# Moving one recurrent group by a slot in two batches of an mLSTM and Fourier-mix kernel

## The chip, the cores and the metric

The kernel runs on one core of one Trainium2 chip. The metric is the device time in microseconds. Three runs of the kernel before took 384.13, 385.11 and 386.57 us, so the median is 385.11 us. The profiled execution took 382.61 us, with a span of 380.7 us.

## The reference

There are two blocks, one behind the other. The first is an mLSTM cell over 4 batches, 8 heads, 768 steps and head size 40. Its result, as 768 rows of 320 features per batch, goes into the second: a Fourier mix over both axes, a normalisation, and an MLP from 320 to 1280 and back with a residual.

```python
for t in range(S):
    m_new = np.maximum(f_gate[:, :, t] + m, i_gate[:, :, t])
    f_stab = np.exp(f_gate[:, :, t] + m - m_new)
    i_stab = np.exp(i_gate[:, :, t] - m_new)
    C = f_stab * C + i_stab * np.einsum('bhd,bhe->bhde', vt, kt)
    n = f_stab * n + i_stab * kt
    y[:, :, t] = sigmoid(o_gate) * (C @ q) / np.maximum(np.abs(n @ q), 1.0)
...
u = x + np.real(np.fft.fft(np.fft.fft(x, axis=1), axis=2))
un = (u - mu) / np.sqrt(var + 1e-06)
return u + np.maximum(un @ w_ch1, 0.0) @ w_ch2
```

## The kernel before, in words

The recurrence is computed in chunks. Each batch has six chunks of 128 steps (c = 0 to 5), and in the batches b = 1, 2, 3 each chunk is cut into two halves of 64 steps. I count batches from one in words: the third batch is b = 2, the fourth b = 3.

All work is put on a list with a slot and a phase, by the function `at`, and is issued in that order: by slot, within a slot by phase. The phases of a slot are EVAC (0), FILL (1), MAIN (2) and FILL_PE (3), plus fractions. So each engine's instruction stream, and that of SP, which issues all loads and stores, is fixed by the list. The engines run their streams in order and wait for each other through semaphores only. A slot is no unit of time: an engine can run ahead of another as far as its waits let it. Batches overlap: while the MLP of one batch runs in the MAIN phases, the recurrence of the next one fills the gaps.

`plan_halves(b, s0)` places the recurrence of a batch from slot s0 on, three slots for each chunk: s = s0 + 3c. The third batch has s0 = 54, the fourth s0 = 86. For a chunk it places:

- loads, six slots ahead: queries and keys (`mlstm_load`, tile qk, three buffers, L518; key and value tile kvt, L520), the matrix of stabilisers W (L529, three buffers, in two transfers) and, in the next slot, the decays Gb (L538). Two slots ahead comes the output gate `so` (L544, four buffers);
- on POOL, two slots ahead, the queries times decays (qg, L563), and one slot ahead the values times weights (vw, L569); in its own slot the mask of W (L578) and the decay of the state (C, L705);
- on ACT, one slot ahead, eight exponentials of W (L551, in two halves of four);
- on TensorE (PE) in its own slot, scores and products to the state (tile ps, all through `product`, L582); three slots later the products from the state and from the chunk (tile ph, L582), on ACT a one-element copy behind the first of them (L748) and the tanh of the gate (L650);
- on DVE, in the slot behind, the state's add (L712) and the weighing of the scores (L717), and later `mlstm_finish` (den L768 to L772, x L759).

Because chunk c's last products stand in the same slot as chunk c+1's first ones, PE meets them as one run of L582 instructions: from the state (c), scores and to the state (c+1), from the chunk (c). This is called a group here. Its products use 64 rows or 40 rows of the array. The group for chunks 3 and 4 is the fifth of a batch, counting the one that holds only chunk 0's first products.

The MLP's first layer (`mlp_block`) runs at the same time for the batch before. It works in five sets (i = 0 to 4) of four slots. Step 0 multiplies into the bank p2, step 1 multiplies with T2 into p1, copies p1 to hidden (L1232) and multiplies into p5. Step 2 multiplies into p3, then with T3 into p1, and copies p1 (L1241). Directly behind it, eight products with 64-row tiles (`rest_products`, L1120) add the features that do not fill 128 rows, with adds to hidden on DVE (L1209). Step 3 begins the next set's p1 (L1203, copied by ACT at L1218) and finishes this one's (L1203, ReLU on ACT at L1254). All other products of a set are L1203 and use 128 rows. ReLUs in place are L1258. A product that accumulates into p1 waits for ACT's copy of p1.

The set i = 0 has slots 63 to 66 for the third batch's recurrence and slots 95 to 98 for the fourth's. Its L1120 products are in slots 65 and 97, the two L1203 of step 3 in 66 and 98. In the kernel before, the group of chunks 3 and 4 stands behind step 3.

Stores of finished rows are L1284 and wait for the residual on DVE (L1281). They stand in SP's stream between the loads.

Of the kernel before, what the change touches and what calls it, by code (L numbers as in the profile page):

```python
# [20 lines left out]
NT = S // L  # L21
NP = H // 2
# [35 lines left out]
def kernel(  # L58
# [68 lines left out]
    def at(slot, phase, fn, *args):  # L127
        plan.setdefault((slot, phase), []).append((fn, args))
# [7 lines left out]
    EVAC, FILL, MAIN, FILL_PE = range(4)  # L136
# [682 lines left out]
    def plan_halves(b, s0, stride=3):  # L819
        at(s0 - 2, FILL + 0.7, halves_start, b)  # L820
        for c in range(NT):
            s = s0 + stride * c
            end = c == NT - 1
            t = 22 + 2 * c if b == 1 and c < 3 else s - 6
            at(t, FILL, mlstm_load, b, c)
            at(t, FILL, mlstm_load_max, b, c)
            at(*((t, FILL + 0.02) if (b, c) == (1, 0) else (t + 1 if c < 2 or b > 1 else s - 5, FILL)), mlstm_load_decay, b, c)
            at(s - 2, FILL, mlstm_load_o, b, c)
            at(s - 2, FILL + 0.1, mlstm_scale_q, b, c)
            at(s - 2, FILL + 0.15, halves_alone, b, c)  # L830
            at(*((s - 3, FILL + 0.06) if (b, c) == (1, 1) else (s - 1, FILL)), mlstm_scale_v, b, c)
            early = (b, c) == (1, 0)
            at(*((27, FILL + 0.227) if early else (s - 1, FILL)), mlstm_exp, b, c, 0)
            at(*((28, FILL + 0.23) if early else (s - 1, FILL + 0.5)), mlstm_exp, b, c, NP)
            at(s, FILL, mlstm_mask, b, c)
            at(s, FILL_PE + 2.05, halves_scores, b, c)
            at(s, FILL_PE + 2.5, halves_to_state, b, c)
            for i in range(2):
                at(s + i, FILL + 0.05, halves_decay, b, c, i)
                at(s + 1 + i, FILL - 0.2, halves_add, b, c, i)  # L840
            at(s + 1, FILL, halves_weigh, b, c)
            if end:
                for fn, phase in (((halves_from_state, -0.3), (halves_between, -0.2), (halves_from_chunk, -0.05)) if b == 1 else
                                  ((halves_from_state, 0.1), (halves_between, 0.15), (halves_from_chunk, 0.3))):
                    at(s + (3 if b == 1 else 4), MAIN + phase, fn, b, c)
            else:
                at(s + 3, FILL_PE, halves_from_state, b, c)
                at(s + 3, FILL_PE + 0.5, halves_between, b, c)
                at(s + 3, FILL_PE + 3, halves_from_chunk, b, c)
            at(s + 3, FILL_PE + 0.6, mlstm_tanh, b, c)  # L850
            at(s + 4, FILL + 0.05 if b == 1 else MAIN + 0.4, mlstm_finish, b, c)

# [565 lines left out]
    def plan_batch(b, s_mlstm, s_mix, s_mlp):  # L1420
        if b == 0:
            plan_mlstm(b)
        else:
            plan_halves(b, s_mlstm)
        done = [s_mlstm + n for n in ((17, 19, 22) if b == 0 else (14, 17, 20))]
        assert s_mix >= done[-1] and s_mlp >= s_mix + 9
        late = [s_mlp + 2 * c for c in range(TG)]
        if b == 0:
            feat = [s_mix + 1, s_mix + 1, s_mix + 2]
            turn = [s_mix + 2, s_mix + 3, s_mix + 4]  # L1430
            add = turn + [s_mix + 5, s_mix + 6, s_mix + 7]
            late = [s_mlp, s_mlp + 1, s_mlp + 2]
        else:
            feat = [s_mix + c for c in ((3, 4, 6) if b == 1 else (3, 4, 7))]
            add = [s_mix + c for c in ((4, 4, 5, 6, 7, 7) if b == 1 else (4, 4, 5, 6, 8, 9))]
            turn = [s_mix + c for c in ((5, 6, 6) if b == 1 else (6, 7, 8))]
            late = [s_mix + c for c in ((7, 8, 8) if b == 1 else (9, 10, 10))]
            at(*((s_mlp, EVAC + 0.5) if b == 1 else (s_mlp - 1, MAIN - 0.05)), mlp_sums)
        plan_mix(b, s_mix, done, feat, add, turn + late)
        s = s_mlp + NFF + 2  # L1440
        at(s, FILL + 0.6, mix_rstd, b)
        for n in range(3):
            at(48 + n if b == 0 else s, FILL + 0.65, mix_rstd_step, b)
        plan_mlp(b, s_mlp)
# [22 lines left out]
    for part, (s, phase) in enumerate(((28, 0.1), (28, 0.11), (28, 0.12))):  # L1467
# [3 lines left out]
    early = [(3, mlstm_load, 3), (3, mlstm_load_o, 2), (4, mlstm_load, 4), (5, mlstm_load_decay, 3),  # L1471
             (5, mlstm_load_decay, 4), (7, mlstm_load_o, 3), (7, mlstm_load, 5),
             (11, mlstm_load_decay, 5), (11, mlstm_load_o, 4), (12, load_tables, None), (15, None, 2),
             (11.5, mlstm_load_o, 5)]
# [157 lines left out]
```

## Time and profile before

| | us |
|---|---|
| timed runs | 384.13, 385.11, 386.57 |
| profiled execution | 382.61 |
| its span | 380.7 |
| PE busy | 374.0 |
| DVE busy | 281.9 |
| ACT busy | 170.5 |
| POOL busy | 132.5 |
| L1203, 128-row products of the first layer: mean of one record | 0.506 |
| L1120, 64-row products: mean of one record | 0.497 |
| one exponential L551: mean | 0.337 |

A product in full precision leaves two matmul records, which overlap, so the pace of products is read from the starts of successive ones and not from the durations. PEld is the loading of weights, which overlaps PE. In a listing in order of time, each row has the start, the duration of the merged run, the engine, the line, the operation, what it writes and reads, and how many instructions are merged; in square brackets stands how long the engine was idle before it and what released it. "issue" means that the profile shows no waiting. SPq rows are the issue of a transfer on SP, not the transfer. In a listing by windows, the columns are the busy time of PE, PEld, DVE, ACT and POOL, the granted clock, the busy share of the DMA engines and GB/s.

### The profile page before, as it was taken

What the parts mean: (1) busy time and instruction counts of PE and PEld (TensorE: products, weight loads), DVE (VectorE), ACT (ScalarE), POOL (GpSimd) and SP (SyncE); (2) the same over time, 40 slices, a digit from 0 to 9 for tenths busy, and PEclk for the clock granted to TensorE, in tenths of its full rate; (3) what the DMA queues carried; (4) which work ended last, traced back from release to release, by engine and by line L of the source; (5) the groups of instructions that cost most, each with busy time, mean ns of one, the idle gap of its engine ahead of it and who ended that gap; (6) DMA issues with size and microseconds to landing.
All of it is one profiled execution on the core that took longest, in us unless ns stands there. A gap on an engine that the chain in (4) does not pass through costs nothing.

```text
span 380.7 us, 11406 instructions
## 1 busy us (share of the span) xinstructions
PE 374.0 (98%) x4602; PEld 275.7 (72%) x4602; DVE 281.9 (74%) x662; ACT 170.5 (45%) x501; POOL 132.5 (35%) x238
## 2 busy tenths in 40 slices
PE   8999999999999999999999999999999999999996
PEld 6788555566677777566588999566588996546996
DVE  7798899999998596787955787877844885246552
ACT  5878768557332224654552054564530233544000
POOL 5666424776595014561602434651300000020000
PEclk9999999999999999999999999999999999999999
DMA  7878499879981344464003644430000001000001
GB/s 217 285 217 310 132 250 250 239 232 261 252 211 37 90 127 128 144 179 131 0 3 94 156 117 138 133 69 3 0 2 34 15 22 36 0 0 2 35 36 34
DMA packets 21760, 43.99 MB, mean 116 GB/s; under 512 B 3508, under 2 KB 9996, under 8 KB 21580
## 3 DMA queue, kind: packets, MB, share of 16 engines
q1 hardware_dynamic: 21708, 43.27, 39.0%
q8 instruction: 36, 0.59, 0.6%
q14 instruction: 16, 0.13, 0.1%
HBM read 39.16 MB, written 4.10 MB: 114 GB/s over the span
## 4 chain that ended last, share of the span: by engine, by line
PE 84%; DVE 4%; POOL 2%; DMA 2%; issue 2%; ACT 1%; SPq 0%; POOLq 0%; DVEq 0%; ACTq 0%
PE po L1332 22%; PE pm L1203 19%; PE po L1275 9%; PE pm L1120 7%; PE ph L582 5%; PE pm L1137 4%; PE ps L582 4%; PE pu L990 3%; PE pz L944 2%; PE put L1039 2%; DMA so<-in_o 2%; PE hb L582 1%; PE pzt L944 1%; PE pz L956 1%; DVE stats L1013 1%
## 5 line engine op out<-in xcount | busy, mean ns | idle before, releaser
L1281 DVE SCALAR_TENSOR_TENSOR x<-po,rstd,x 128x160 f32<-128x160 f32 (+1 forms) x69 | 27.1, 394 | 36.6 <-PE po L1332 34.0
L1209 DVE TENSOR_TENSOR h<-h,pm 128x384 f32<-128x384 f32 x60 | 30.5, 549 | 24.7 <-PE pm L1120 11.4
L578 POOL TENSOR_SCALAR_AFFINE_SELECT W<-W 64x512 f32<-64x512 f32 x36 | 27.7, 769 | 38.0 <-ACT W L551 28.6
L1203 PE MATMUL pm<-uT,w_sb 128*128 128x384 f32 x90 | 37.5, 506 | 0.1
L705 POOL TENSOR_TENSOR C<-C,decB 128x164 f32<-128x164 f32 x33 | 19.1, 578 | 52.0 <-DVE C L712 48.7
L551 ACT ACTIVATE W<-W,colT 128x64 f32<-128x64 f32 x144 | 36.6, 337 | 0.0
L1275 PE MATMUL po<-w_sb,h 128*128 128x320 f32 x120 | 33.9, 433 | 0.0
L1120 PE MATMUL pm<-uT,w_sb 64*64 64x384 f32 x320 | 33.7, 497 | 0.0
L563 POOL TENSOR_TENSOR qg<-qk,Gb 128x512 f32<-128x512 f32 x21 | 27.3, 1302 | 8.4 <-DMA Gb<-G_d 7.7
L1063 POOL TENSOR_TENSOR t<-rstd 128x6 f32<-128x6 f32 x12 | 3.7, 312 | 76.1 <-DVE v L1057 75.6
L1275 PEld LDWEIGHTS po<-w_sb,h 128*128 128x128 f32 x120 | 22.4, 190 | 9.1 <-issue 0.3
L1137 PE MATMUL pm<-uT,w_sb 128*128 128x384 f32 x80 | 28.6, 498 | 0.0
L1332 PE MATMUL po<-T,S 128*128 128x160 f32 x180 | 27.8, 301 | 0.2 <-DVE x L1281 0.2
L1332 PEld LDWEIGHTS po<-T,S 128*128 128x128 f32 x180 | 25.4, 190 | 1.3 <-DVE x L1281 0.4
L1332 PE MATMUL po<-w_sb,h 128*128 128x160 f32 x180 | 26.3, 300 | 0.0
L1332 PEld LDWEIGHTS po<-w_sb,h 128*128 128x128 f32 x180 | 25.2, 190 | 1.4 <-DVE x L1281 0.3
L1203 PEld LDWEIGHTS pm<-uT,w_sb 128*128 128x128 f32 x90 | 15.5, 189 | 12.8 <-DVE h L1209 5.3
L1258 ACT ACTIVATE h<-h 128x384 f32<-128x384 f32 x45 | 23.1, 520 | 2.9 <-DVE h L1209 2.9
L1120 PEld LDWEIGHTS pm<-uT,w_sb 64*64 64x64 f32 x320 | 11.4, 132 | 16.9 <-issue 13.7
L1137 PEld LDWEIGHTS pm<-uT,w_sb 128*128 128x128 f32 x80 | 14.2, 190 | 10.5 <-issue 1.8
L569 POOL TENSOR_TENSOR vw<-kvt,colT 128x328 f32<-128x328 f32 x23 | 19.6, 851 | 4.8 <-DVE colT L289 2.5
L582 PE MATMUL ps<-qk 40*64 40x64 f32 (+1 forms) x768 | 19.2, 235 | 0.0
(254 smaller groups left out, 820.4 us busy)
## 6 DMA issues: line engine op xcount, KB each, us to landing
kvt<-in_kv SPq DMA_DIRECT2D x24, 336.0 KB
qk<-in_qkT SPq DMA_DIRECT2D x48, 160.0 KB
raw<-in_w SPq DMA_DIRECT2D x10, 640.0 KB
Gb<-G_d SPq DMA_DIRECT2D x42, 128.0 KB
W<-M_d SPq DMA_DIRECT2D x36, 128.0 KB
so<-in_o SPq DMA_DIRECT2D x24, 160.0 KB
out<-x SPq DMA_DIRECT2D x23, 160.0 KB
ds_sb<-in_dft_s SPq DMA_DIRECT2D x1, 1158.0 KB
```

The costliest lines, as they stand in the source:

```text
L551: nc.scalar.activation(out=k.W[:, h, :], in_=M, func=AF.Exp, scale=-1.0, bias=colT[:, c, 0, b * H + h:b * H + h + 1])
L563: nc.gpsimd.tensor_tensor(out=k.qg[:, :, t], in0=k.qk[:, 0, :, t], in1=k.Gb[:, :, t], op=OP.mult)
L578: nc.gpsimd.affine_select(out=W, in_=W, compare_op=OP.is_ge, fill=0.0, base=base, pattern=[[0, H], [-1 if back else 1, LH]], channel_multi ...
L582: nc.tensor.matmul(out, w, x, start=start, stop=True, skip_group_check=True)
L1120: nc.tensor.matmul(banks[i][half(cols)], w1_rest(n)[half(i), half(cols)], u[half(i)], start=start, stop=not start, skip_group_check=True)
L1137: nc.tensor.matmul(k.pm[i], w1_block(ch, f // 2 * 2 + i), u[2 * ch], start=(ch == 0 and not ahead), stop=(ch == 1 and (ahead or n in (2, 8 ...
L1203: nc.tensor.matmul(bank, w, u, start=start, stop=True, skip_group_check=True)
L1209: nc.vector.tensor_tensor(out=h, in0=h, in1=bank, op=OP.add)
L1258: nc.scalar.activation(out=h, in_=h, func=AF.Relu, scale=-1.0)
L1275: nc.tensor.matmul(k.po[m], hidden(gr, f)[:, i * L:(i + 1) * L], w2_sb[:, f, :], start=(f == 0), stop=(f == NFF - 1))
L1281: nc.vector.scalar_tensor_tensor(out=u, in0=po, scalar=k.rstd[:, c:c + 1], in1=u, op0=OP.mult, op1=OP.add)
L1332: nc.tensor.matmul(po, a[:, f], w[:, f], start=start and f == 0, stop=f == half - 1, skip_group_check=True)
```

## The change

For the third and fourth batch (b > 1) only:

- Chunk 4 (c = NT - 2) goes one slot sooner as a whole (s is one less): its loads, scalings, mask, scores, products to the state and state adds.
- The last products of chunk 3, its tanh and its finish go one slot sooner with it, so that the group of chunks 3 and 4 stays one group. It stands in slot 65 (97), behind the L1120 products and ahead of the two L1203 of step 3. The last products, tanh and finish of chunk 4 keep their old slots.
- The exponentials of chunk 4 go from s - 1 to two slots ahead of its new s, into the FILL_PE phase of slot 63 (95), and those of chunk 5 from slot 68 (100) to four slots ahead, the FILL_PE phase of slot 65 (97).

```diff
-            s = s0 + stride * c
+            s = s0 + stride * c - (b > 1 and c == NT - 2)
             end = c == NT - 1
+            follow = s + 3 + (b > 1) * ((c == NT - 2) - (c == NT - 3))
...
-            at(*((27, FILL + 0.227) if early else (s - 1, FILL)), mlstm_exp, b, c, 0)
-            at(*((28, FILL + 0.23) if early else (s - 1, FILL + 0.5)), mlstm_exp, b, c, NP)
+            ahead = (s - (2 if c == NT - 2 else 4), FILL_PE + 0.7) if b > 1 and c >= NT - 2 else None
+            at(*((27, FILL + 0.227) if early else ahead or (s - 1, FILL)), mlstm_exp, b, c, 0)
+            at(*((28, FILL + 0.23) if early else ahead or (s - 1, FILL + 0.5)), mlstm_exp, b, c, NP)
...
-                at(s + 3, FILL_PE, halves_from_state, b, c)
-                at(s + 3, FILL_PE + 0.5, halves_between, b, c)
-                at(s + 3, FILL_PE + 3, halves_from_chunk, b, c)
-            at(s + 3, FILL_PE + 0.6, mlstm_tanh, b, c)
-            at(s + 4, FILL + 0.05 if b == 1 else MAIN + 0.4, mlstm_finish, b, c)
+                at(follow, FILL_PE, halves_from_state, b, c)
+                at(follow, FILL_PE + 0.5, halves_between, b, c)
+                at(follow, FILL_PE + 3, halves_from_chunk, b, c)
+            at(follow, FILL_PE + 0.6, mlstm_tanh, b, c)
+            at(follow + 1, FILL + 0.05 if b == 1 else MAIN + 0.4, mlstm_finish, b, c)
```

In the streams of the engines this gives, in each of the two batches: on PE the group passes the two L1203 of step 3. On ACT chunk 4's exponentials pass L1232 and stand behind chunk 2's tanh; chunk 3's copy L748 and tanh and then chunk 5's exponentials pass L1218, L1254 and L1258. On POOL qg and vw of chunk 4 pass the decay of chunk 3's second half. On DVE chunk 4's first state add and weighing pass one weight sum, in the third batch only. On SP the Gb loads of chunk 4 pass chunk 3's gate load and, in the third batch, a store too; the gate load of chunk 4 passes the query, key/value and W loads of chunk 5. The numbers of instructions are the same on every engine.

## The prediction

> **What bounds the kernel.** I read the table of busy time first, then the chain that ended last, then the timeline around slots 64 to 69 of the third batch (b = 2) and 96 to 101 of the fourth (b = 3).
>
> ```profile
> span 380.7 us, 11406 instructions
> PE 374.0 (98%) x4602; PEld 275.7 (72%) x4602; DVE 281.9 (74%) x662; ACT 170.5 (45%) x501; POOL 132.5 (35%) x238
> PE 84%; DVE 4%; POOL 2%; DMA 2%; issue 2%; ACT 1%; SPq 0%; POOLq 0%; DVEq 0%; ACTq 0%
> ```
>
> TensorE is busy 98% of the span and holds 84% of the chain; the granted clock is 9 tenths or more in every slice. Listed in order of time, the chain stays on PE from 257.80 us to the end. So the change is worth what it takes from or adds to PE's own sequence. The two places look alike; this is the fourth batch:
>
> ```profile
> 243.55 2.02 ACT L551 ACTIVATE W<-W,colT 128x64 f32<-128x64 f32 x8
> 244.55 2.30 PE L1120 MATMUL pm<-uT,w_sb 64*64 64x384 f32 x16
> 245.47 0.46 ACT L1241 COPY h<-pm 128x384 f32<-128x384 f32 x1
> 245.98 0.20 PEld L1120 LDWEIGHTS pm<-uT,w_sb 64*64 64x64 f32 x6 [0.60 <-ACT h L1241]
> 246.78 0.30 PEld L1203 LDWEIGHTS pm<-uT,w_sb 128*128 128x128 f32 x2 [0.60 <-DVE h L1209]
> 248.27 0.56 PEld L582 LDWEIGHTS ph<-C,qg 40*64 40x64 f32 x32 [0.55 <-issue]
> 249.90 2.00 ACT L551 ACTIVATE W<-W,colT 128x64 f32<-128x64 f32 x8
> 250.15 0.91 PE L1203 MATMUL pm<-uT,w_sb 128*128 128x384 f32 x2
> ```
>
> The reader is to see ACT's order. The eight exponentials of chunk 4 (243.55) stand ahead of the copy L1241. That copy waits only for a product of 243.71, so it could start at about 244.56 (in an undisturbed set the product is at 168.81 and the copy at 169.66, 0.85 later). It starts at 245.47, and the 64-row products L1120 wait for it. Then come two 128-row products, the recurrent group, and the next 128-row product at 250.15. The third batch has the same picture at 160.52 to 166.13.
>
> **What leaves PE's path.** The order of instructions shows one change on PE in each of the two batches: the two L1203 products go from before the group to behind it. Nothing is added or removed on any engine. From the first L1120 to the L1203 that follows all of this, PE now takes 166.13 - 160.52 = 5.61 us and 250.15 - 244.55 = 5.60 us. Afterwards I add: L1120 to the group's first product as where they already stand side by side, 1.34 us (169.55 to 170.89, next fence); the group, 164.24 to 166.13, 1.89; the first 128-row product behind a group, 166.13 to 166.88, 0.75; the second at the running pace, 0.65 (167.52 to 168.17). Sum 4.63, so **0.98 us less in the third batch and 0.97 in the fourth**.
>
> ```profile
> 169.55 1.55 PE L1120 MATMUL pm<-uT,w_sb 64*64 64x384 f32 x16
> 170.89 0.65 PE L582 MATMUL ph<-C,qg 40*64 40x41 f32 x32
> ```
>
> Of it 0.77 is the wait for the copy (L1120 to the next L1203 takes 1.47 in a quiet set, 185.01 to 186.48, here 2.24) and 0.2 the saved change between 128-row and 64-row products. The first part comes from chunk 4's exponentials alone: they go to right behind the tanh of 156.48 (and 240.55), where ACT now idles 2.21 us (2.16) until L1232. They would run 156.95 to 158.97 and 241.0 to 243.0; L1232 is ready at 159.15 and 243.18, so 0.2 us of slack covers them. Their W was issued at 146.18 and 233.44, long before.
>
> For the change of shape the rows give 0.1 us a side: a running product takes 0.64 (168.17 to 168.81), the last one ahead of 64 rows 0.74 (168.81 to 169.55) and the first behind them 0.75, although the weight load idles 0.55 there. One change each way goes per batch.
>
> The Trainium skill (TensorEngine Tiling (Array Packing), Key Properties) says that changing the tiling mode drains TensorE. It states no price; were the drain the whole idle of 0.55, each side would save 0.45 more, 1.8 in both batches, and the sum below would be 383.3. The pace of the products is against it.
>
> **What else moves.** On POOL the query scaling (1.26) and the value scaling (0.74) of chunk 4 pass the decay of chunk 3's second half. They wait for the group of slot 63, which is done with its queries at 156.4; then 157.0 to 159.2, the decay to 159.7, the mask to 161.1. The adds that read this stand at 161.70 on DVE, the group needs the values at about 162.9. Hidden by 1 to 2 us; without that cover the group would wait the difference. DVE's three adds L1209 stand at 161.93 and now have until 163.75, when the first L1203 comes. The add and the weighing of chunk 4 pass a 1.04 us weight sum in the third batch, whose result is first used in the second layer's products, at 193.55. The decay load Gb of chunk 4 is issued ahead of a store and of chunk 3's gate load; the gate is read 10 us later.
>
> **What becomes late.** Chunk 5's eight exponentials go four slots ahead, in front of L1218, L1254 and L1258. They need chunk 5's W. In the same edit the gate load of chunk 4 (L544, 160 KB) goes ahead of chunk 5's query, key/value and W loads on SP. In the third batch, W is issued at 157.79 and the trace's landing semaphores end at 161.39. The exponentials can start at about 163.2 (tanh behind the group's first part). With the gate load ahead, up to 0.85 later, it is still there in time: they end at 165.2, L1218 at 165.6, and the product that needs it (the second of the next set, at 165.8) waits for nothing. The fourth batch differs:
>
> ```profile
> 236.92 5.42 SPq L1284 DMA_DIRECT2D out<-x  x2
> 242.39 0.75 SPq L518 DMA_DIRECT2D qk<-in_qkT  x2
> 243.19 0.35 SPq L520 DMA_DIRECT2D kvt<-in_kv  x1
> 243.70 1.09 SPq L529 DMA_DIRECT2D W<-M_d  x2
> 244.84 0.59 SPq L544 DMA_DIRECT2D so<-in_o  x1
> ```
>
> ```profile
> 245.00:245.50 0.50, 0.50 (x9) 0.19 (x2) 0.47 (x2) 0.50 (x4) 0.00 (x0) 1.00 1.01 254
> 249.00:249.50 0.50, 0.50 (x59) 0.50 (x51) 0.00 (x0) 0.44 (x3) 0.00 (x0) 1.00 0.97 212
> ```
>
> SP sits on a store until 242 (it waits for L1281 on DVE), and only then issues chunk 5's loads, in one burst. The second fence, half-microsecond windows with the DMA share as the last figure but one, shows the DMA engines full from 245 to 249.5. The landing semaphores of W's two halves end at 248.62 and **249.28**, those of the gate load behind them at 250.12. So today's exponentials at 249.90 have W by 0.6 us. Moved, they would reach ACT's head at 247.2 (group from 245.89, its first results 0.8 later, tanh to 247.2) and stand there for W, with L1218 behind them. The gate load put ahead of W adds between 0.4 (its issue alone; 0.42 to 0.59 in the rows) and 0.84 us (what it takes behind W). I take 0.7, near the upper end since the engines are full: W at 249.98. The Trainium skill (DMA: Bandwidth & Descriptors, Queues, rings and completion order) says that each DMA engine consumes descriptors in ring order, so this load delays W; the landing order here agrees, 249.28 before 250.12.
>
> The exponentials take 2.0, the next ACT row starts 0.1 ahead of their end (245.57 against 245.47): L1218 at 251.88, done 252.36, the waiting product at 252.41 (0.05 later, as at 159.63 to 159.68). It now starts at 250.90 and without the wait would start at 249.93. So the wait costs 2.48 and leaves **+1.51 us** there. Some comes back: the next 64-row products now wait for a DVE add (253.57) behind a 1.47 us gate product that POOL's qg slows; L1120 to the L1203 after the next group is 257.73 - 253.57 = 4.16 against 173.15 - 169.55 = 3.60. DVE will have done that gate product before 250, so 0.56 goes. Net **+0.95 in the fourth batch**.
>
> **Sum.** -0.98 + 0.95 = -0.03 us: no change. The profiled execution took 382.61 us (span 380.7), the timed runs 385.11 in the median (384.13 to 386.57), 2.5 above it; on that scale I forecast **385.1**. Bounds: gate load without effect on W, 384.4; 0.84 and nothing of the 0.56 back, 385.8. About 1% (3.9 us) is what a measurement here tells from no change.
>
> **Rivals.**
> - *Chunk 5's W is not late in the fourth batch*: -0.98 - 0.97 - 0.56 = -2.5, 382.6 us. For it: the cost hangs on one burst, and a store issued some 2 us sooner would end it. Against it: 249.28 is 2 us behind 247.2, and DVE's order ahead of the store is unchanged. 0.17.
> - *The backlog is larger (slower)*: the gate load moves at the slowest pace of the burst (139 GB/s at 246.5, 1.2 us for 160 KB), W lands at 250.5, and the 0.56 does not come back as L1254, L1258 and L1232 queue on ACT: -0.98 + 1.51 + 0.5 = +1.0, and with L1232 one copy late (0.5) +1.5, 386.6 us. It decides from a landing after 250.1. 0.2.
> - *No gain from the move*: another wait takes the copy's place (the add L1209 for the first L1203, slack 1.3; L1232 behind the exponentials, slack 0.2). Then -0.98 goes, +1.9, 387.0. Little speaks for it: 0.05.
>
> The forecast has 0.58. The range 382.6 to 387.0 takes in the rivals and the scatter of the runs. None of the cases reaches 3.9 us by itself; for the scatter I leave faster by over 1% 0.05, slower 0.05, within 0.9.
>
> **What would show it.** Right: L1120 in both batches without the 0.60 wait for L1241 and L582 straight behind it; in the fourth batch ACT idle for some 2.7 us ahead of L551 with a DMA named as releaser, and the second product of the next set waiting for ACT. The step on W falls if that idle is missing; the first step falls if L1120 still takes 2.30. The whole is wrong if a wait appears outside these two places, above all in the mixing of the batch.

## The result, and the profile after

The changed kernel is slower by 0.58%: the ratio of its times to those of the kernel before is 1.0058, with an interval of 1.0031 to 1.0085. The median of 20 runs is 386.50 us, that of 20 runs of the kernel before 383.69 us, so the change costs about 2.2 us (1.2 to 3.3). The ratio leaves out a few runs in a second, slower state, so it is not the ratio of these two medians. The three runs from which I forecast had a median of 385.11 us. On the larger set of runs "no change" would have been 383.7 us, so the median lies inside the range of 382.6 to 387.0 us partly because that range stood too high.

The page of the profiled execution after: the span, the busy times, and the shares of the chain that ended last.

```profile
span 384.0 us, 11410 instructions
...
PE 373.0 (97%) x4602; PEld 275.2 (72%) x4602; DVE 281.4 (73%) x662; ACT 170.4 (44%) x501; POOL 132.1 (34%) x238
...
PE 73%; DVE 8%; issue 5%; POOL 3%; ACT 3%; DMA 1%; SPq 1%; POOLq 0%; ACTq 0%; DVEq 0%
```

TensorE does 1.0 us less (373.0 against 374.0), and the span is 3.3 us longer. In the chain, PE's share falls from 84% to 73%; "issue" grows from 2% to 5% and DVE from 4% to 8%. So there are new waits, and not all of them are on a semaphore.

In the code after the change, lines from L1120 on are higher by two: L1120 is now L1122, L1203 is L1205, L1209 is L1211, L1218 is L1220, L1232 is L1234, L1284 is L1286 and L1303 is L1305. In the experiments they are as after, but in e3 higher by one and in e9 by three.

To see where the time goes I take the distances between the first L1120 product of successive MLP sets. In the third batch's recurrence I call the first three sets a, b, c, and in the fourth's d, e, f. Predicted was -0.98 for a to c and +0.95 for d to f.

| us | start of a | a to b | b to c | a to c | d to e | e to f | d to f |
|---|---|---|---|---|---|---|---|
| before | 160.52 | 9.03 | 8.80 | 17.83 | 9.03 | 9.35 | 18.38 |
| after | 162.65 | 8.44 | 9.54 | 17.98 | 10.59 | 8.80 | 19.39 |

The 3.3 us of the span have three parts: 2.13 ahead of a, 0.15 in the third batch and 1.01 in the fourth. From c to d nothing moved (66.20 and 66.19). The fourth batch does what was predicted. The third does not, and nothing was predicted for the part ahead of it.

**The third batch.** The timeline of the kernel after, in order: TensorE and its weight loads.

```profile
162.65 1.52 PE L1122 MATMUL pm<-uT,w_sb 64*64 64x384 f32 x16
164.49 0.56 PEld L582 LDWEIGHTS ph<-C,qg 40*64 40x64 f32 x32 [0.99 <-DVE x L759]
164.50 0.68 PE L582 MATMUL ph<-C,qg 40*64 40x41 f32 x32 [0.32 <-DVE x L759]
166.38 0.91 PE L1205 MATMUL pm<-uT,w_sb 128*128 128x384 f32 x2
171.88 0.21 PEld L1122 LDWEIGHTS pm<-uT,w_sb 64*64 64x64 f32 x8 [0.60 <-DVE h L1211]
```

The 64-row products now run through in 1.52 us instead of 2.30, and the group comes right behind them. But the group starts 1.84 us behind the first L1122, where the sum had 1.34: its first product waits for L759, the end of the finish of chunk 2. And the next set, which was undisturbed before, waits for a DVE add (171.88). The same stretch on DVE and POOL, after, and then four rows of before:

```profile
159.57 1.51 DVE L1193 TENSOR_TENSOR m<-uT,raw 128x384 f32<-128x384 f32 x1
162.93 0.98 DVE L772 SCALAR_TENSOR_TENSOR so<-so,den 128x320 f32<-128x320 f32 x1
163.95 0.49 DVE L759 TENSOR_TENSOR x<-ph,so 128x320 f32<-128x320 f32 x1
166.96 2.10 DVE L1305 TENSOR_TENSOR w_sb<-w_sb 128x800 f32<-128x800 f32 x1
```

```profile
159.09 1.58 POOL L563 TENSOR_TENSOR qg<-qk,Gb 128x512 f32<-128x512 f32 x1
162.21 1.37 POOL L578 TENSOR_SCALAR_AFFINE_SELECT W<-W 64x512 f32<-64x512 f32 x2
166.94 1.27 POOL L563 TENSOR_TENSOR qg<-qk,Gb 128x512 f32<-128x512 f32 x1
```

```profile
157.44 0.56 DVE L1191 TENSOR_TENSOR m<-uT,raw 128x384 f32<-128x384 f32 x1
160.76 0.49 DVE L772 SCALAR_TENSOR_TENSOR so<-so,den 128x320 f32<-128x320 f32 x1
163.34 1.04 DVE L1303 TENSOR_TENSOR w_sb<-w_sb 128x800 f32<-128x800 f32 x1
161.61 1.38 POOL L578 TENSOR_SCALAR_AFFINE_SELECT W<-W 64x512 f32<-64x512 f32 x2 [0.78 <-ACT W L551]
```

Three DVE operations take about twice as long or more, each beside a POOL operation that it did not stand beside before: L1193 takes 1.51 us (before 0.56, with POOL idle from 156.99 to 158.32), the gate product L772 0.98 (before 0.49, with POOL idle from 160.83 to 161.61), the weight sum 2.10 (before 1.04). In the first case the change moved POOL's query scaling there; in the second the mask, which comes sooner because chunk 4's exponentials do; in the third it moved the weight sum itself, on DVE, beside chunk 5's query scaling. All three read two tensors in SBUF. One that reads a tensor from SBUF and the other from a bank that TensorE has written keeps its time: the product L759 takes 0.49 us at 163.95, with POOL idle, and 0.49 at 170.64 beside a mask. The second slow operation delays L759 and so the group; the third delays the adds of the next set.

**The fourth batch.** The timeline of SP, ACT and PE:

```profile
239.20 5.41 SPq L1286 DMA_DIRECT2D out<-x  x2
246.45 1.09 SPq L529 DMA_DIRECT2D W<-M_d  x2
```

```profile
246.82 1.52 PE L1122 MATMUL pm<-uT,w_sb 64*64 64x384 f32 x16
249.57 1.06 PE L582 MATMUL ph<-kvt,W 64*64 64x41 f32 x32
252.20 2.02 ACT L551 ACTIVATE W<-W,colT 128x64 f32<-128x64 f32 x8 [2.62 <-DMA W<-M_d]
254.63 0.91 PE L1205 MATMUL pm<-raw 128*128 128x384 f32 x2 [1.87 <-ACT h L1220]
```

ACT stands idle for 2.62 us until W has landed, and the second product of the next set waits for L1220 behind the exponentials. It starts 7.81 us behind the first L1122; the prediction had 7.86 (252.41 less 244.55). One row was not foreseen: the group's last products (249.57) take 1.06 us instead of 0.66.

**Ahead of both.** A window of the kernel after, between 80 and 90 us, where the instruction streams of both kernels are the same, and below it the same window of before. The columns are the window, its length, the busy time (and instructions) of PE, PEld, DVE, ACT and POOL, the granted clock, the DMA share and GB/s. Then two rows of PE's timeline after:

```profile
80.00:90.00 10.00, 8.19 (x156) 4.83 (x154) 7.58 (x15) 3.30 (x9) 6.15 (x9) 1.00 0.75 209
80.00:90.00 10.00, 10.00 (x166) 5.75 (x168) 9.50 (x18) 5.28 (x16) 7.25 (x10) 1.00 0.79 229
```

```profile
81.32 1.50 PE L1122 MATMUL pm<-uT,w_sb 64*64 64x384 f32 x10 [0.63 <-issue]
87.75 0.54 PE L582 MATMUL ph<-kvt,W 64*64 64x41 f32 x18 [1.18 <-issue]
```

TensorE is busy for 8.19 of 10 us at full clock (before: 10.00). Twice it stops in the middle of a run of products and waits for nothing that the profile shows ("issue").

### The profile page after: what moved, and what is told of

It reads as the page before. It is cut to its first block, busy times and chain, and to the rows that moved or that the text cites. A ratio compares the mean times of both kernels' runs of the same rounds, so it can differ in the third digit from the quotient of the medians.

```text
span 384.0 us, 11410 instructions
## 1 busy us (share of the span) xinstructions
PE 373.0 (97%) x4602; PEld 275.2 (72%) x4602; DVE 281.4 (73%) x662; ACT 170.4 (44%) x501; POOL 132.1 (34%) x238
## 4 chain that ended last, share of the span: by engine, by line
PE 73%; DVE 8%; issue 5%; POOL 3%; ACT 3%; DMA 1%; SPq 1%; POOLq 0%; ACTq 0%; DVEq 0%
PE po L1334 19%; PE pm L1205 16%; PE po L1277 7%; PE pm L1122 6%; PE pm L1139 4%; PE ph L582 4%; PE ps L582 3%; PE pu L992 3%; PE pz L946 2%; PE hb L582 2%; ACT W L551 2%; DMA W<-M_d 1%; PE pzt L946 1%; DVE stats L1015 1%; POOL W L578 1%
## 5 line engine op out<-in xcount | busy, mean ns | idle before, releaser
L1211 DVE TENSOR_TENSOR h<-h,pm 128x384 f32<-128x384 f32 x60 | 30.5, 550 | 27.1 <-PE pm L1205 13.7
L578 POOL TENSOR_SCALAR_AFFINE_SELECT W<-W 64x512 f32<-64x512 f32 x36 | 28.4, 788 | 36.4 <-ACT W L551 25.2
L551 ACT ACTIVATE W<-W,colT 128x64 f32<-128x64 f32 x144 | 36.6, 335 | 2.6 <-DMA W<-M_d 2.6
L1205 PE MATMUL pm<-uT,w_sb 128*128 128x384 f32 x90 | 37.3, 503 | 0.1
L705 POOL TENSOR_TENSOR C<-C,decB 128x164 f32<-128x164 f32 x33 | 18.2, 550 | 49.7 <-DVE C L712 45.4
L1122 PE MATMUL pm<-uT,w_sb 64*64 64x384 f32 x320 | 32.7, 496 | 0.6 <-issue 0.6
L1205 PEld LDWEIGHTS pm<-uT,w_sb 128*128 128x128 f32 x90 | 15.7, 189 | 12.1 <-DVE h L1211 4.1
L1122 PEld LDWEIGHTS pm<-uT,w_sb 64*64 64x64 f32 x320 | 11.1, 132 | 16.8 <-issue 14.5
```

Of the source, the lines that this page charges most:

```text
L551: nc.scalar.activation(out=k.W[:, h, :], in_=M, func=AF.Exp, scale=-1.0, bias=colT[:, c, 0, b * H + h:b * H + h + 1])
L578: nc.gpsimd.affine_select(out=W, in_=W, compare_op=OP.is_ge, fill=0.0, base=base, pattern=[[0, H], [-1 if back else 1, LH]], channel_multi ...
L1122: nc.tensor.matmul(banks[i][half(cols)], w1_rest(n)[half(i), half(cols)], u[half(i)], start=start, stop=not start, skip_group_check=True)
L1205: nc.tensor.matmul(bank, w, u, start=start, stop=True, skip_group_check=True)
L1211: nc.vector.tensor_tensor(out=h, in0=h, in1=bank, op=OP.add)
```

## The experiments

The theory after this reading: the group's gain is halved by DVE being slowed beside POOL; W costs what was predicted; the part ahead of a does not come from the moved work. The rivals: the moved exponentials are the cause; the gate load and not the store makes W late; the moved work reaches back to 80 us in some way. All ratios are to the kernel before, measured on the same chip; distances are of the profiled executions.

**The changed kernel again**, with no edit.

> The changed kernel once more, to separate the scatter from the effect. Theory A: the two distances are 17.98 and 19.39 us again within 0.2, and the median is 1 to 2 us above that of before on the same chip. Rival B: the first L1120 of the third batch is again more than 1.5 us later than in the kernel before (160.52), and the whole 2 us slower or more.

Ratio 1.0090 (1.0049 to 1.0130). Start of a 163.77, a to c 17.98, d to f 19.05. The "issue" stops are there again (1.59 us at 82.16 and 1.17 at 88.60, at the same two instructions). So they are no accident of one execution of this program.

**e1: chunk 5's exponentials at their old place**

```diff
-ahead = (s - (2 if c == NT - 2 else 4), FILL_PE + 0.7) if b > 1 and c >= NT - 2 else None
+ahead = (s - 2, FILL_PE + 0.7) if b > 1 and c == NT - 2 else None
```

> The changed kernel with chunk 5's exponentials back in slots 68 and 100; the rest of the change stays. Theory A (what the two traces show at the two places): the wait of ACT for W in the fourth batch goes, and with it 1.93 us on PE (there the product behind L1220 came 3.73 late after 1.80). Left are +0.15 in the third batch, -0.47 in the fourth and there perhaps -0.55 (a DVE add no longer late), so 0.3 to 0.9 us less than the kernel before. Rival B (the loss sits in the 2.1 us which the profiled execution of the changed kernel was late at 107 us already, ahead of the first moved instruction, and belongs to the change): still 1 to 2 us slower than before.

Ratio 0.9997 (0.9957 to 1.0038); a to b 9.39, d to e 9.96, d to f 18.77. The weight loads of TensorE in the third batch:

```profile
169.92 0.30 PEld L1205 LDWEIGHTS pm<-e,raw 128*128 128x128 f32 x2 [1.29 <-ACT h L1234]
```

With the group sooner, TensorE reaches the next set before ACT has done the exponentials at their old place, and the copy L1234 stands behind them. So this part of the change is needed by the other, where W is there in time: from a to b it is worth 0.95 us in the third batch (9.39 against 8.44). Up to c only 0.21 is left (18.19 against 17.98), since behind the longer wait the late weight sum no longer delays the next set (b to c 8.80). I had expected 0.3 to 0.9 us less than the kernel before, and that did not come.

**e2: the gate load of chunk 4 behind chunk 5's loads again**

```diff
-at(s - 2, FILL, mlstm_load_o, b, c)
+at(s - 2 + (b > 1 and c == NT - 2), FILL, mlstm_load_o, b, c)
```

> The changed kernel with chunk 4's gate load issued behind chunk 5's query, key/value and W loads again, as before the change; chunk 5's exponentials stay ahead. Theory A with the prediction's 0.7 for the gate load: W lands 0.4 to 0.84 us sooner in the fourth batch, and ACT's idle time ahead of L551 there shrinks from 2.62 to about 1.9 (1.8 to 2.2), the time by as much: 0.4 to 0.8 us less than the changed kernel. Rival: the burst is bound by something else, the landing stays, no difference.

Ratio 1.0017 (0.9978 to 1.0055); a to c 17.98, d to f 19.00. ACT idles 2.23 us ahead of L551, with 2.62 in the kernel after and 2.28 when that kernel ran again. Behind the first L1122 the waiting product starts at 7.41 us. In the kernels that leave SP's order here as the change has it, it starts at 7.46 (the changed kernel again), 7.81, 7.86 (e5), 8.26 (e7, below) and 8.94 (the padded kernel, below). The gate load's share, 0.4 to 0.84 us by my estimate, is lost in the scatter of W's landing, and putting it back does not cure the wait.

**e3: the kernel before with chunk 4's exponentials alone moved**

```diff
+ahead = (s - 3, FILL_PE + 0.7) if b > 1 and c == NT - 2 else None
-at(*((27, FILL + 0.227) if early else (s - 1, FILL)), mlstm_exp, b, c, 0)
+at(*((27, FILL + 0.227) if early else ahead or (s - 1, FILL)), mlstm_exp, b, c, 0)
```

(and the same in the line for the other four heads)

> The kernel before with chunk 4's exponentials alone moved to the FILL_PE phase of slots 63 and 95; no group moves. The prediction's step (0.77 us of the 0.98 come from these exponentials alone): 0.77 in each batch, 1.5 us less than before. Theory A (DVE is late as well: the adds L1209 stand behind chunk 2's finish, at 161.93 and 245.98 in the trace of before, whoever is ahead on ACT): the first L1203 still waits until the first of these adds is done, 246.47, so at 246.5 in place of 246.78: 0.25 in each batch, 0.5 less than before.

Ratio 0.9968 (0.9934 to 1.0002); a to b 9.32, so 0.29 longer; d to e 9.13, 0.10 longer; d to f 17.93, 0.45 shorter, all of it in the next set (e to f 8.80). Weight loads and DVE in the third batch:

```profile
162.66 0.30 PEld L1204 LDWEIGHTS pm<-uT,w_sb 128*128 128x128 f32 x2 [1.67 <-DVE h L1210]
```

```profile
160.38 1.00 DVE L772 SCALAR_TENSOR_TENSOR so<-so,den 128x320 f32<-128x320 f32 x1
```

The wait for the copy is gone, and nothing is gained at the place: the two products of step 3 now wait for the adds of the 64-row products, which stand on DVE behind a gate product of 1.00 us. The mask L578, which follows the exponentials, starts at 160.39 here and at 161.61 before. So the gain that I put down to the exponentials alone takes the group's move as well, which gives DVE that time.

**e4 and e5: the change in the third batch alone, and in the fourth alone** (`b > 1` becomes `b == 2`, or `b == 3`, in the three new expressions)

> The whole change in the third batch alone. Prediction: -0.98. Theory A: -0.49 at the group (which waits for chunk 2's finish on DVE) and +0.74 in the next set (whose 64-row products wait for a DVE add behind a weight sum that takes 2.10 in place of 1.04 beside POOL), +0.15 in sum with the rounding of the rows, no difference that can be measured. Rival B: +1 to +2 us, though the fourth batch is as before.

> The whole change in the fourth batch alone. Theory A: the distance from the first L1120 of the batch's first set to that of its third grows from 18.38 to about 19.4 us, 1.0 us slower than before in all. Rival B (the loss belongs to streams ahead of the moved instructions): 2 us slower or no difference, by chance, with the same 1.0 at the place.

e4: ratio 1.0008 (0.9967 to 1.0049), a to c 17.98, d to f 18.48. e5: 1.0040 (1.0001 to 1.0079), a to c 17.83, d to f 19.45. The two places add up (0.15 in e4's third batch and 1.07 in e5's fourth are 1.22, against 1.16 for both), and a starts at 160.37 and 159.83: with either half of the change alone, no time is lost ahead of it. (e1 and e2, which have nearly all of it, lie between: 161.38 and 161.27.)

**e6: chunk 5's loads in the fourth batch one slot sooner, ahead of the second store**

```diff
-t = 22 + 2 * c if b == 1 and c < 3 else s - 6
+t = 22 + 2 * c if b == 1 and c < 3 else s - 6 - ((b, c) == (3, NT - 1))
```

> The changed kernel with chunk 5's query, key/value and W loads of the fourth batch issued ahead of the second of the two stores that SP waits for (and so ahead of chunk 4's gate load). Theory A (W is late only since SP sits on that store until 242 and then issues everything in one burst): W is issued as soon as chunk 2's products release its buffer, lands about 3 us sooner, ACT's idle time of 2.62 us ahead of L551 goes and with it 1.9 us on PE: 18.38 us becomes about 17.5, and the whole is 1.9 us faster than the changed kernel, some 0.8 faster than before. Rival (the DMA engines are full in any case): the idle time stays above 1.5.

Ratio 0.9967 (0.9931 to 1.0003); d to f 17.55, which is 1.84 less than after and 0.83 less than before. SP and ACT in the fourth batch:

```profile
237.07 0.76 SPq L518 DMA_DIRECT2D qk<-in_qkT  x2
...
241.57 1.40 SPq L529 DMA_DIRECT2D W<-M_d  x2
243.06 0.53 SPq L1286 DMA_DIRECT2D out<-x  x1
```

```profile
246.96 2.00 ACT L551 ACTIVATE W<-W,colT 128x64 f32<-128x64 f32 x8
```

W is issued 2.7 us ahead of d (244.30) and no longer 0.4, and the exponentials start without idle time ahead of them. So the wait in the fourth batch came from SP, which sat on a store while the load stood behind it.

**e7: POOL's scaling of chunk 4 back behind the state decay, the third batch's weight sum from slot 66 to 77**

```diff
+own = int(b > 1 and c == NT - 2)
-at(s - 2, FILL + 0.1, mlstm_scale_q, b, c)
+at(s - 2 + own, FILL + 0.1, mlstm_scale_q, b, c)
...
-at(66 if n == 3 else 57, FILL + 0.41, out_weight_sums, n)
+at(77 if n == 3 else 57, FILL + 0.41, out_weight_sums, n)
```

(the same `+ own` for `halves_alone` and `mlstm_scale_v`)

> The changed kernel with POOL's query and value scalings of chunk 4 behind the decay of chunk 3's second half again, as before the change, and the weight sum in slot 77 in place of 66. Theory A (DVE is slowed by POOL beside it, and its lateness takes half of the gain in the third batch and gives a stall in its next set): the last of the four operand sums on DVE (L1193, 1.51 us) is back at 0.56, the group's wait for the finish L759 shrinks from 0.99 to 0.6 or less of the weight load's idle time, the stall of 0.60 in the next set goes, and the distance of the third batch falls from 17.98 to 16.9 to 17.3 us (17.83 before the change). The fourth batch keeps its wait for W. In all 0.7 to 1.0 less than the changed kernel. Rival (the group waits for something else): 17.9 or more.

Ratio 1.0030 (0.9991 to 1.0070). L1193 is back to 0.56 us and b to c to 8.80, so a to c is 17.23, 0.60 less than in the kernel before. But a to b stays at 8.43: the group still waits for L759, because the gate product is still slow beside the mask, now its first half (1.01 us from 160.00, the mask from 160.02). So the slow L1193 cost the group next to nothing; the slow gate product makes the wait. In the slot 77 the weight sum delays another set by 0.3, and in the fourth batch, which still has SP's order, d to f is 19.83.

**The padded kernel: the changed kernel with one more instruction on POOL** (a one-element memset, 0.09 us at 273.8 us, long behind everything in question)

```diff
+at(112, FILL + 0.9, nc.gpsimd.memset, warm[64:65, 2:3], 0.0)
```

> The changed kernel with one more instruction: a memset of one spare element on POOL, near the end of the fourth batch's MLP; TensorE, VectorE, ScalarE and SyncE have the same instructions in the same order. It is to tell whether the microsecond or two that the changed kernel loses ahead of the third batch's recurrence belongs to the moved work. Theory (it does not; it comes from how the program is supplied to TensorE, which any small alteration changes): the distances of the sets stay at 17.98 and 19.0 to 19.4 us, the stalls of TensorE on nothing but the issue between 80 and 90 us are gone or elsewhere, the first set of the third batch's recurrence starts at 159.8 to 161.5 us, and the time is 1 to 1.5 us over the kernel before (ratio 1.002 to 1.004). Rival (the moved work causes it): start at 162.6 to 163.8 us again, stalls at 80 to 90 us again, ratio 1.006 to 1.009.

Ratio 1.0011 (0.9975 to 1.0047). a starts at 160.31, a to c is 17.97, d to f 20.52. The windows of this kernel between 80 and 90 us:

```profile
80.00:90.00 10.00, 10.00 (x170) 6.00 (x172) 9.68 (x19) 5.59 (x16) 7.57 (x10) 1.00 0.79 228
```

TensorE is busy for all of it and the stops are missing, while the third batch shows the same distance. The interval lies just below that of the changed kernel's second run, but overlaps that of its first (1.0031 to 1.0085), so the traces tell the two kernels apart and the times hardly do. They were not on the same chip; but on the chip of that second run e5, e6 and e7 have their a at 159.8 to 160.1, so it isn't the chip alone. The moved work is therefore not enough to make the 2 to 3 us ahead of a: with all of it in place and an instruction more, they are not there in this execution.

The 20.52 missed the expectation of 19.0 to 19.4, because W landed later:

```profile
250.98 2.02 ACT L551 ACTIVATE W<-W,colT 128x64 f32<-128x64 f32 x8 [3.76 <-DMA W<-M_d]
```

From the issue of W to these exponentials it takes 6.90 us here (244.08 to 250.98) and 5.75 in the kernel after (246.45 to 252.20), and the product behind L1220 starts at 8.94 instead of 7.81. PE's rows ahead of it show something else, which costs nothing here, as that product waits longer still:

```profile
247.21 0.52 PE L582 MATMUL ph<-kvt,W 64*64 64x41 f32 x21
248.96 0.43 PE L582 MATMUL ph<-kvt,W 64*64 64x41 f32 x11 [1.23 <-issue]
```

This is the same kind of stop as at 81 and 88 us, inside the moved group. In the fourth batch the step to the 118th of the group's 128 products takes 0.34 us in the kernel after, 0.07 when it ran again, and in e1, e2, e6, e7 and the padded kernel 0.92, 1.18, 0.64, 0.56 and 1.45; in e5 it is 0.03, and the next one 0.07. Before, no step near there is over 0.03. The third batch's group has it in none of these runs, nor has the fourth's where it stands as before (before, e3 and e4). So the stop lies at one place of TensorE's stream, and its length differs. The same holds for the earlier ones: e2 stops for 0.62 us at 86.52, at the very product of the stop at 87.75 in the kernel after. Counting all instructions that the trace has of TensorE in order, the stops at 81.32, 87.75 and in the group are at 2241, 2497 and 7360: 256 and 19 times 256 apart, to within one. A stop of 0.29 us in e1 and e3 (at 105.33 and 104.17) is at 3265, 3 times 256 behind the second.

**e8: both repairs, e6 and e7, together**

> Changed kernel with both repairs: the last chunk's loads of the fourth batch one slot sooner, ahead of the second store, and POOL's products of the fifth group behind its second decay again, with the third batch's sum of output weights moved from slot 66 to slot 77. If the two repairs are independent: first to third set 17.2 us in the third batch (before 17.83) and 17.5 or less in the fourth (before 18.38), 0.3 us lost at slot 77, so 1.2 us less than the kernel before: ratio 0.996 to 0.998. If DVE's or POOL's later work takes the place of the waits in the fourth batch (there W is in time only if POOL's products are too), 18 us or more there and a ratio of 0.999 to 1.001.

Ratio **0.9948** (0.9908 to 0.9988), median 381.63 against 383.80; a to c 16.71, c to d 66.46, d to f 17.41. The third batch is better than expected by 0.5. The next two kernels tell why.

**e8b: as e8, the weight sum in a gap of DVE at the end of slot 82**

```diff
-at(77 if n == 3 else 57, FILL + 0.41, out_weight_sums, n)
+at(*((82, FILL_PE + 1) if n == 3 else (57, FILL + 0.41)), out_weight_sums, n)
```

> As the kernel with both repairs, but the third batch's sum of output weights (0.99 us on DVE) goes to the end of slot 82, where the trace shows DVE idle for 1.33 us behind the last ReLU of the MLP's input and ahead of the hidden sums. Expected: the 0.3 us between the last set and the fourth batch's recurrence comes back (66.2 instead of 66.5), and the rest is as in the kernel with both repairs: 1.5 us less than before, ratio 0.995 to 0.997. If the gap is needed by what follows it, the first output products wait instead, 66.5 us or more again.

Ratio 0.9974 (0.9947 to 1.0000). The 0.3 us from c to d came back (66.19), as expected. But a to c is 17.23 and d to f 17.96. In the fourth batch the stop inside the group is 1.18 us here and 0.62 in e8. In the third the gate product differs; its row in e8 first, then in e8b:

```profile
160.44 0.49 DVE L772 SCALAR_TENSOR_TENSOR so<-so,den 128x320 f32<-128x320 f32 x1
```

```profile
160.57 1.01 DVE L772 SCALAR_TENSOR_TENSOR so<-so,den 128x320 f32<-128x320 f32 x1
```

In both, POOL's mask starts just behind it: 25 ns in e8, 22 in e8b (12 in e3, 20 in e7, and L772 took 1.00 and 1.01 there). In e8 the mask's first half takes 0.98 us, elsewhere 0.65. In the fourth batch, where the mask starts 111 to 116 ns behind the gate product (e3, e7, e8, e8b), the gate product keeps its 0.51 us and the mask's first half takes 0.91. So one of the two is held up by the other, and at 12 to 25 ns a few nanoseconds go with which one.

**e9: as e8b, two one-element memsets on POOL ahead of the mask, third batch only**

```diff
+for i in range(2 * (b == 2) * own): at(s, FILL, nc.gpsimd.memset, warm[64:65, 2 + i:3 + i], 0.0)
 at(s, FILL, mlstm_mask, b, c)
```

> The kernel with both repairs and the sum of output weights at the end of slot 82, and with two one-element memsets on POOL (0.09 us each in the padded run) ahead of the fifth group's mask in the third batch, so that POOL's mask starts some 0.2 us behind DVE's gate product instead of within 0.02 us of it. Theory (whichever of DVE's gate product and POOL's mask starts first holds the other up, and the group's first product waits for DVE's finish behind the gate product): the gate product takes 0.49 to 0.51 us instead of 1.01, and the first to second set of the third batch 7.9 us instead of 8.43, first to third 16.7 instead of 17.2. Rival (the 0.5 us between 7.91 and 8.43 in the two kernels with both repairs comes from the place of the weight sum, or from chance elsewhere): 8.43 us again whatever the gate product takes. Fourth batch as it is, 17.4 to 18.0. Time 1.5 to 2 us less than before, ratio 0.995 to 0.997.

Ratio **0.9950** (0.9908 to 0.9992), median 380.72 against 382.88; a to b 7.91, a to c 16.71, c to d 66.19, d to f 17.41. DVE, POOL and PE in the third batch:

```profile
160.92 0.49 DVE L772 SCALAR_TENSOR_TENSOR so<-so,den 128x320 f32<-128x320 f32 x1
```

```profile
161.25 1.39 POOL L578 TENSOR_SCALAR_AFFINE_SELECT W<-W 64x512 f32<-64x512 f32 x2
```

```profile
160.68 1.52 PE L1123 MATMUL pm<-uT,w_sb 64*64 64x384 f32 x16
162.02 0.65 PE L582 MATMUL ph<-C,qg 40*64 40x41 f32 x32
```

The mask starts 0.33 us behind the gate product, neither is slowed (the mask's halves take 0.67 and 0.66), and the group follows the 64-row products at 1.34 us, as in the sum. The theory's two numbers (7.9 and 16.7) came, and the rival's (8.43) did not. e8 and e9 beat both the kernel before and the changed one; their intervals do not tell one from the other.

## Why the prediction was wrong

I forecast -0.03 us; the interval is +1.2 to +3.3. In the profiled executions the miss is 3.3 us: 1.13 in the third batch (+0.15 in place of -0.98), from the step on POOL and DVE below; 0.06 in the fourth; and 2.13 ahead of both, for which the prediction had no term.

**What leaves PE's path (4.63 us): right as a length, wrong as a forecast.** The product that the sum ends at comes 5.12 us behind the first L1122 in the third batch after (167.77 less 162.65), and 4.59 in e9 (165.27 less 160.68). So the durations were right, 0.1 us for the change of shape included. That speaks against the other value that I weighed: with 0.45 more saved a side, e9 would have come 0.9 sooner. What was missing is the wait of the group's first product. I took its start from a row where DVE had finished long before (170.89). At the new place the finish of the chunk before ends at the very moment that the group arrives, and 0.5 us of DVE decides 0.5 us of the kernel.

**"The first part comes from chunk 4's exponentials alone": wrong.** e3 has them alone, and TensorE waits for DVE's adds instead, 0.29 us longer than before in the third batch and 0.10 in the fourth. The sign stood in the prediction's own rows: the first L1203 (246.78) is released there by DVE's L1209 and not by the copy. This did not move the sum, since the change has both parts.

**"Hidden by 1 to 2 us" (POOL and DVE): the step that failed.** I compared when the moved POOL work had to be done with when it would be done. I did not ask what runs beside it. POOL's query scaling, mask and value scaling now lie beside DVE operations that read two tensors in SBUF, and those took 1.51 instead of 0.56, 0.98 instead of 0.49, and 2.10 instead of 1.04 us. I had the mask end at 161.1, and the gate product stood at 160.76: the overlap was in my own numbers. The price in the third batch is 0.49 at the group and 0.74 at the next set, against a gain of 0.98 and 0.10 that I had not counted (the next set's first product no longer stands behind the group: 0.65 instead of 0.75). The sum is +0.15 in the place of -0.98. The weight sum, which I named as passed and free, was the dearest of them. e7 takes away the second price (b to c 8.80), e9 the first as well (a to b 7.91). The prediction had such a case before it: it says of the next set's gate product that "POOL's qg slows" it, and used this only where it brought a gain.

The Trainium skill (SBUF — State Buffer, SBUF: two separate sides) has the rule: VectorE and GpSimd share a pair of SBUF ports under an exclusive lock, and whichever starts first holds it for the whole instruction, between a VectorE operation with two SBUF inputs and a GpSimd operation that reads SBUF too. The runs agree that one waits for the other: beside the mask the gate product ends about 0.34 us behind the half that it waits for (in e8b the half ends at 161.25, the gate product at 161.59), and where it is ahead by 25 ns (e8) or by 111 to 116 (the fourth batch) the mask is the one to be held up. At less they don't show who was first: in e3, e7 and e8b the gate product is ahead by 12 to 22 ns on record, and still the slow one.

**Chunk 5's exponentials in the third batch: right.** No wait appeared for them there. e1 shows that at the old place they would have cost 0.95 up to b, and 0.21 up to c.

**What becomes late in the fourth batch: right in size.** Predicted was a wait that leaves +1.51 us at the second product of the next set, and 0.56 back behind it. Measured: that product is 7.81 us behind the first L1122, before it was 6.35, so +1.46; and e to f went from 9.35 to 8.80, so 0.55 came back. The net is +1.01 where I had +0.95. e6 shows the cause, the store that SP sits on. That the number came so close is luck: with the same order on SP the product starts at 7.46 to 8.94. The gate load, to which I gave 0.7 us of it, can't be told from the scatter (e2).

**The group in the fourth batch: a term that was missing.** The group has its own stop of 0.07 to 1.45 us at a fixed place. In the changed kernel the wait for W hides it, since the product behind waits longer anyway. Where W is in time it shows: in e9 the fourth batch takes 8.61 from d to e, the third 7.91 from a to b, and the stop is 0.63. That is why the repaired kernel gains 1.12 us in the third batch and 0.97 in the fourth, of which 0.55 is the next set.

**"A wait appears outside these two places": it did.** 2.13 us of the profiled execution (3.25 in the second one) were lost ahead of the third batch's recurrence, in streams that the change left alone. The padded kernel, e6 and e7 have the moved instructions and not this loss. So of the 3.3 us between the profiled executions, 1.16 belongs to the two places, and 2.13 to the program as it was built, which the moved work alone does not bring; the timed runs, at +2.2, lie between the two. The trace suggests what it is: the stops lie 256 places of TensorE's stream apart, or multiples of that, they wait for no semaphore, and the DMA records have 36 packets of 16 KB of the kind "instruction", and 256 goes 36 times into the 9300 instructions that the trace has of TensorE. In this stretch they stand at 78.6, 85.2 and 89.3 us in the kernel after, against 78.1, 83.0 and 88.4 before. That points to instructions that arrive late. It is argued from the trace and not shown by a run, and the packets may also come later because TensorE does. Why one program stops at some of these places and another, with the same stream up to there, does not, stays open.

**The rivals.** "No gain from the move" (0.05) was nearest: another wait did take the copy's place, but at the group and not at the add, and through DVE being slowed, which I had not thought of. Its +1.9 lies near the measured +2.2 by luck, as 2.13 us came from elsewhere. "The backlog is larger" did not happen in the changed kernel (product at 7.81), though in the padded one (8.94) it did. "W is not late" became true only with e6.

## What to carry to other kernels

When an edit moves work of POOL or DVE, list what the other of the two will be doing at that time; an operation of DVE that reads two tensors in SBUF took two to three times as long there, and a deadline that is met on paper is missed by that much. When a wait is taken away, look for the second-latest releaser of the same instruction and for its margin: here it was the finish behind a gate product with 20 ns between it and a mask. And before a difference of 0.5% is put down to an edit, look for time lost in streams that the edit left alone; the same kernel with a one-element memset far behind helps to tell the two apart.

## What the runs showed that I had not expected

- A DVE product of two SBUF tensors beside POOL: 0.49 becomes 0.98 to 1.01 us, 0.56 becomes 1.51, 1.04 becomes 2.10. With starts 12 to 25 ns apart, either engine lost: 0.98 instead of 0.65 us for half a mask where POOL did.
- TensorE stops with no semaphore to wait for, at places of its stream that lie multiples of 256 instructions apart, for 0.07 to 1.59 us. In one program they come at 81 to 82 and at 88 us in both profiled executions; with one instruction more far behind, they did not.
- The landing of W in the fourth batch scatters by 1.5 us between kernels with the same order of transfers: from its issue to the exponentials 5.42 to 6.90 us, at a DMA share of 0.75 to 1.07 in the three microseconds behind the issue.
